# A recurrence and two dense layers on one core: a weight block loaded in halves, and a new order of the work

## The chip, the cores and the metric

The kernel runs on one core of a Trainium2 chip. The metric is device time in microseconds (us) of one execution; the time before is the median of three runs, 177.47 us (177.21 to 177.65). TensorE (PE) multiplies matrices into eight PSUM banks, VectorE (DVE), ScalarE (ACT) and GpSimd (POOL) do the elementwise work, and SyncE (SP) issues the transfers between the chip's memory (HBM) and the on-chip buffers (SBUF).

## The reference

```python
# q, k, v, f_logit: (4, 8, 768, 48) float32; w_in: (384, 2048); w_out: (2048, 384)
f = 1.0 / (1.0 + np.exp(-f_logit))
for t in range(S):
    state = f[:, :, t, :, None] * state + np.einsum('bhd,bhe->bhde', k[:, :, t], v[:, :, t])
    y[:, :, t] = np.einsum('bhd,bhde->bhe', q[:, :, t], state)
x = y.transpose(0, 2, 1, 3).reshape(B * S, H * D)      # (3072, 384)
h = x @ w_in
out = np.maximum(0.01 * h, h) @ w_out
```

The state of each of 32 heads decays by its own gate per element and step; the result goes through two dense layers with a leaky relu between.

## The kernel before

Time is cut into six chunks of 128 steps. The work comes in twelve units: units 0 to 3 are the first two chunks of one batch each (two steps in a pair share a row of the tiles), units 4 to 11 are one later chunk of two batches each. For each unit, and for each half `a` of it:

- f, k, q and v are loaded by SP (`Lf`, `Lk`, `Lq`, `Lv`; half a paired unit is 192 KB).
- ACT makes e = exp(-f) (`ge`, L229) and its logarithm lf (`gl`, L241); TensorE sums lf over time in PSUM (`cs`, L250 to L261); ACT makes the growth and decay factors em, at and end of it (`dec`, L274 to L280).
- DVE or POOL scale k and q by them (`k`, `q`, L286); v is cast on POOL (`v`, L291 to L300). TensorE turns k and q (`tk`, `tq`, L319), and DVE or ACT copy them out of PSUM (`ck`, `cq`); from unit 3 on a DMA transposes (`xk`, `xq`).
- TensorE makes the scores (`sc`, L355, L362), DVE masks them (`mk`, L372, L376), and TensorE mixes them with v and the last state (`mx`, `ms`, L393). The state's update is `pt` (L458, L463) on TensorE, `sf` (L473 to L480) on DVE, `sb` (L483) on POOL.
- ACT or DVE copy the mix out as xT (`xt`, L445, L447). TensorE multiplies it by w_in: `up` for one unit of 256 rows and 256 columns of w_in (six matmuls, L510), `uw` for a pair of units of 512 rows and 128 columns (three matmuls, L521). ACT applies the leaky relu (`pr` L516, `pw` L525); `dn` (L532) multiplies by a quarter of w_out, four matmuls at a time; the result is copied (`ob`) and stored (`st`).

Both weights are read in quarters into staging buffers, which are raw_fk4, raw_qv4, raw_fk5 and raw_qv5, the same that later hold the inputs of units 4 and 5, and cast to bfloat16 from there. `WI` and `WO` load a whole quarter (768 KB); `CI` and `CO` cast a third of it (128 x 512). `We_i_x` loads half x of w_in's quarter i (256 of its columns, 384 KB), and `Ce_i_x_y` casts 128 columns of it. A cast's last number is the engine: 0 DVE, 1 ACT, 2 POOL; elsewhere a last 1 is POOL (or ACT for copies out of PSUM).

All of this stands in one list of words, `order`, from L582 on; nothing else sets the order. Each word calls one of the functions in `parts`, and each engine runs its own words in the list's order, waiting for what they need; a word's bank of PSUM stands behind the @, so `up_0_4@6` is the fifth up of unit 0 into bank 6, which must have been read out by then. SP's words are its transfers in order. `F_n@b` puts n units of filler on TensorE (L135): two units are one matmul of 128 x 512 of a constant, an odd last one 128 x 256. Nobody reads them.

```python
    def fill(n, bank):
        for a in range(0, n, 2):
            m = 2 * min(2, n - a)
            nc.tensor.matmul(banks[bank][:, 0:128 * m].rearrange("t (a n) -> t a n", a=m), filler,
```

Of the kernel before, what the change touches and what calls it, by code (L numbers as in the profile page):

```python
# [15 lines left out]
def kernel(  # L16
# [665 lines left out]
```

## Time and profile before

| what | us |
|---|---|
| median of three runs | 177.47 (177.21 to 177.65) |
| the profiled execution | 176.78 |
| its span, first to last instruction | 175.0 |
| TensorE busy | 167.8 |
| ACT busy | 104.5 |
| DVE busy | 85.5 |
| POOL busy | 72.6 |
| fillers on TensorE (24 of 512 columns, 5 of 256) | 8.8 + 1.5 |

The page gives busy times per engine, the chain of work that ended last, and groups of instructions by line. A busy TensorE counts overlapping, pipelined matmuls, so a matmul's listed length is longer than its place in a row of them. The 1.78 us between the span and the time of the execution lie outside the instructions.

### The profile page before, as it was taken

The numbers are of one execution on the slowest core, as the hardware profiler recorded it, in microseconds if no ns is written. First come the engines' busy times: TensorE is split into PE (matmuls) and PEld (weight loads), VectorE is DVE, ScalarE is ACT, GpSimd is POOL, SyncE is SP. The second block draws the span as 40 slices with busy tenths as digits, with TensorE's granted clock in tenths as the row PEclk, the third lists the DMA queues.
The fourth block names the chain that finished last, engine by engine and source line by source line (L and its number), as shares of the span: only waits on it lengthen the run. The fifth ranks groups of instructions, "written<-read, shape, count | busy, mean of one in ns | idle before, by whom it ended". The sixth has DMA issues, their size and how long they took to land.

```text
span 175.0 us, 5158 instructions
## 1 busy us (share of the span) xinstructions
PE 167.8 (96%) x2101; PEld 105.6 (60%) x2101; DVE 85.5 (49%) x170; ACT 104.5 (60%) x228; POOL 72.6 (41%) x153
## 2 busy tenths in 40 slices
PE   7788899999999999999999999999999999999993
PEld 2555678887656776754555754566644565644672
DVE  4198886637439805761235680957720238600030
ACT  5873955899634681279963579910689910466501
POOL 7669776466701061530291646901601938000000
PEclk9999999999999999999999999999999999999999
DMA  5999999989999999988999999999989599040022
GB/s 142 267 284 312 358 307 328 365 265 280 202 186 179 123 236 194 184 184 175 229 220 145 267 194 189 208 148 205 246 183 228 109 194 276 9 184 0 0 90 90
DMA packets 110535, 34.93 MB, mean 200 GB/s; under 512 B 102960, under 2 KB 109744, under 8 KB 110512
## 3 DMA queue, kind: packets, MB, share of 16 engines
q1 hardware_dynamic: 110512, 34.61, 86.8%
q8 instruction: 16, 0.26, 0.6%
q14 instruction: 7, 0.06, 0.1%
HBM read 25.17 MB, written 4.72 MB: 171 GB/s over the span
## 4 chain that ended last, share of the span: by engine, by line
PE 85%; SPq 5%; DMA 3%; DVE 3%; issue 1%; POOL 0%; ACT 0%; POOLq 0%; DVEq 0%
PE ps L532 35%; PE ps L521 24%; PE ps L510 11%; SPq L164 5%; PE ps L393 5%; DMA raw_qv<-in_q_dram 3%; PE ps L362 3%; PE ps L548 2%; PE ps L258 1%; PE ps L463 1%; DVE wm L372 1%; PE ps L319 1%; DVE kh L286 1%; PE ps L355 1%; PE ps L261 1%
## 5 line engine op out<-in xcount | busy, mean ns | idle before, releaser
L532 PE MATMUL ps<-w_out,gT 128*128 128x384 bf16 x368 | 65.5, 326 | 0.0
L532 PEld LDWEIGHTS <-gT 128*128 128x128 bf16 x368 | 34.4, 98 | 23.0
L521 PE MATMUL ps<-xT,w_in 128*128 128x512 bf16 x192 | 44.1, 379 | 0.0
L525 ACT ACTIVATE gT<-ps 128x512 bf16<-128x512 f32 x64 | 35.1, 629 | 8.2 <-PE ps L521 7.9
L521 PEld LDWEIGHTS <-w_in 128*128 128x128 bf16 x192 | 18.3, 98 | 20.3 <-issue 0.2
L376 DVE TENSOR_TENSOR wm<-ps,ut 128x512 bf16<-128x512 f32 x32 | 19.9, 684 | 14.4 <-PE ps L362 8.2
L510 PE MATMUL ps<-xT,w_in 128*128 128x256 bf16 x192 | 22.8, 273 | 0.0
L445 ACT CAST xT<-ps 128x384 bf16<-128x384 f32 x13 | 6.3, 520 | 25.8 <-PE ps L393 25.8
L543 DVE COPY osb<-ps 128x384 f32<-128x384 f32 x15 | 8.2, 555 | 26.5 <-PE ps L532 21.7
L291 POOL CAST vb<-raw_qv 128x384 bf16<-128x384 f32 (+1 forms) x16 | 11.0, 690 | 24.5 <-DMA raw_qv<-in_v_dram 21.7
L516 ACT ACTIVATE gT<-ps 128x512 bf16<-128x512 f32 x32 | 17.3, 623 | 5.0 <-PE ps L510 5.0
L510 PEld LDWEIGHTS <-w_in 128*128 128x128 bf16 x192 | 18.2, 98 | 2.6
L286 DVE TENSOR_TENSOR qh<-raw_qv,at 128x768 bf16<-128x768 f32 (+1 forms) x10 | 9.4, 944 | 19.0 <-DMA raw_qv<-in_q_dram 16.4
L286 POOL TENSOR_TENSOR kh<-raw_fk,em 128x768 bf16<-128x768 f32 (+1 forms) x6 | 10.6, 1759 | 17.9 <-ACT em L274 9.6
L483 POOL CAST sb<-sf 64x192 bf16<-64x192 f32 x40 | 14.1, 353 | 8.8 <-DVE sf L473 6.7
L274 ACT ACTIVATE em<-ps 128x384 bf16<-128x384 f32 x24 | 12.7, 530 | 7.8 <-PE ps L261 7.0
L229 ACT ACTIVATE e<-raw_fk 128x384 f32<-128x384 f32 (+1 forms) x16 | 10.8, 683 | 9.8 <-DMA raw_fk<-in_f_logit_dram 9.8
L475 DVE TENSOR_TENSOR sf<-sf,ps 64x192 f32<-64x192 f32 x32 | 11.2, 351 | 5.4 <-PE ps L463 4.5
L286 DVE TENSOR_TENSOR kh<-raw_fk,em 128x384 bf16<-128x384 f32 (+1 forms) x10 | 8.2, 825 | 9.7 <-ACT em L274 9.5
L275 ACT ACTIVATE at<-ps 128x384 bf16<-128x384 f32 x24 | 12.9, 536 | 0.0
L286 POOL TENSOR_TENSOR qh<-raw_qv,at 128x384 bf16<-128x384 f32 (+1 forms) x6 | 7.6, 1259 | 11.5 <-DMA raw_qv<-in_q_dram 9.1
L480 POOL TENSOR_TENSOR sf<-sf,end 128x192 f32<-128x192 f32 x16 | 9.2, 573 | 7.4 <-ACT gT L525 5.9
(88 smaller groups left out, 191.4 us busy)
## 6 DMA issues: line engine op xcount, KB each, us to landing
out_dram<-osb SPq DMA_DIRECT2D x23, 192.0 KB, 2.6
raw_fk<-in_f_logit_dram SPq DMA_DIRECT2D x22, 192.0 KB, 3.9
raw_qv<-in_v_dram SPq DMA_DIRECT2D x22, 192.0 KB, 3.9
raw_fk<-in_k_dram SPq DMA_DIRECT2D x22, 192.0 KB, 4.1
raw_qv<-in_q_dram SPq DMA_DIRECT2D x22, 192.0 KB, 4.1
raw_fk<-in_moe_w_out_dram SPq DMA_DIRECT2D x2, 768.0 KB, 8.8
raw_qv<-in_moe_w_out_dram SPq DMA_DIRECT2D x2, 768.0 KB, 7.3
raw_fk<-in_moe_w_in_dram SPq DMA_DIRECT2D x1, 768.0 KB, 5.9
```

The lines of the kernel that those rows point to most:

```text
L274: nc.scalar.activation(ems[j % 2][:, a], t[:, 0:H * D], AF.Exp, scale=1.0)
L275: nc.scalar.activation(ats[j % 2][:, a], t[:, 0:H * D], AF.Exp, scale=-1.0)
L286: eng.tensor_mul(heads(j, to[j % NR], a)[:, :, :, 0:D], raw_heads(j, x, a), decays(j, by, a))
L291: nc.gpsimd.tensor_copy(out=heads(j, vb, a), in_=raw_heads(j, "v", a))
L376: nc.vector.tensor_mul(w, src.rearrange("t (p n) -> t p n", p=P2), ut[:, None, :].to_broadcast([128, P2, 128]))
L475: nc.vector.tensor_add(sf[rows], sf[rows], new)
L483: nc.gpsimd.tensor_copy(out=sb[rows, :, y * D:y * D + D], in_=sf[rows])
L510: nc.tensor.matmul(pm[:, i, :], w_in_of(ff, kk), xTs[j // 2 % 2][:, kk, j % 2].rearrange("t a s -> t (a s)"), start=(kk == 0), stop=(kk == ...
L516: nc.scalar.activation(dst, pm, AF.Prelu, alpha=0.01)
L521: nc.tensor.matmul(banks[bank], w_in_of(ff, kk), xTs[j // 2 % 2][:, kk].rearrange("t u a s -> t (u a s)"), start=(kk == 0), stop=(kk == NK ...
L525: nc.scalar.activation(g_blocks(j)[ff], banks[st[j].pop(("pm", ff))], AF.Prelu, alpha=0.01)
L532: nc.tensor.matmul(po, g_of(j, ff, a), w_out_b[quarter][:, ff % 4, :], start=(ff == 0), stop=(ff == NF - 1))
```

## The change

Only the list `order` changes; the functions are the same. The third quarter of w_in (`WI_2`, cast by `CI_2_x`) is now loaded in two halves and cast in four pieces, and its first half is the first of all weights to be loaded:

```diff
-WI_2
-CI_2_0_2 CI_2_1_2 CI_2_2_1
+We_2_0 We_2_1
+Ce_2_0_1_2 Ce_2_0_0_1 Ce_2_1_0_2 Ce_2_1_1_2
```

(These words are gathered here from their places in the list.) The rest of the list is drawn anew: the same words of every other kind and in the same numbers, in another order, with other banks and with some scalings, copies and casts on other engines. Six of 16 scalings of k were POOL's and now eight are; of q six were and now three. The pair mask goes from POOL to DVE. The fillers shrink from 53 units to 41:

```diff
-F_19@1 F_4@2 F_1@4 F_2@0 F_4@5 F_6@6 F_2@5 F_4@6 F_2@5 F_4@3 F_2@2 F_1@7 F_1@4 F_1@1
+F_15@1 F_2@3 F_2@5 F_3@1 F_1@2 F_2@6 F_1@0 F_1@0 F_6@6 F_4@0 F_1@0 F_1@2 F_1@4 F_1@2
```

The start of the list:

```diff
     order = """
-    c0 Lf_0_1 ge_0_1 Lf_0_0 Lv_0_1 Lf_1_1 gl_0_1 Lk_0_1 Lq_0_1 zk_1 zk_0 F_19@1 cs_0_1@0 zk_2 zv_2_0 ge_0_0 gl_0_0
-    Lv_0_0 dec_0_1 zv_0_0 ge_1_1 Lk_0_0 zv_1_0 q_0_1_0 Lq_0_0 zs_2_1 pm_1 gl_1_1 k_0_1_0 F_4@2 cs_0_0@1 cs_1_1@2
-    F_1@4 tq_0_1@3 Lf_1_0 Lk_1_1 Lq_1_1 tk_0_1@4 zs_1_1 dec_0_0 v_0_1 Lk_1_0 dec_1_1 Lv_1_1 ge_1_0 v_0_0 q_1_1_1
-    Lv_1_0 cq_0_1_1 k_0_0_0 Lf_2_0 Lq_1_0 q_0_0_0 tk_0_0@5 gl_1_0 Lf_2_1 ck_0_0_0 ck_0_1_0 WI_2 F_2@0 pt_0_2@6.7
-    v_1_1 v_1_0 sf_0_0 tq_0_0@0 zs_0_1 k_1_1_0 F_4@5 sc_0_1@1.2 cs_1_0@5 cq_0_0_1 tk_1_1@4 mk_0_1_1 F_6@6 tq_1_1@3
-    Lq_2_1 dec_1_0 mk_0_1_0 sc_0_0@6.0 q_1_0_1 sb_0_0 k_1_0_0 We_0_0 mk_0_0_1 We_1_1 mk_0_0_0 Lk_2_1 cq_1_1_0 ge_2_1
...
+    c0 zv_0_0 Lf_0_1 Lf_0_0 ge_0_1 Lk_0_1 Lf_1_1 gl_0_1 zk_0 Lq_0_1 Lk_0_0 Lq_1_1 F_15@1 cs_0_1@0 ge_0_0 zk_1 pm_0
+    gl_0_0 Lq_0_0 zs_2_0 zs_3_1 dec_0_1 k_0_1_0 Lf_2_1 ge_1_1 Lv_0_0 cs_0_0@1 Lf_1_0 Lv_0_1 Lf_2_0 Lk_1_1 dec_0_0
+    gl_1_1 q_0_1_0 q_0_0_1 We_2_0 Lk_1_0 Lq_1_0 Lv_1_0 Lv_1_1 F_2@3 tk_0_1@2 tq_0_1@3 ge_2_1 Lk_2_1 gl_2_1 k_0_0_0
+    zk_2 F_2@5 tk_0_0@4 zs_1_0 cq_0_1_0 cs_1_1@5 dec_1_1 ck_0_0_0 ck_0_1_0 ge_1_0 Lq_2_0 v_0_0 We_2_1 tq_0_0@6
+    cq_0_0_0 F_3@1 sc_0_1@7.0 sc_0_0@1.3 q_1_1_0 ge_2_0 v_0_1 k_1_1_1 mk_0_1_0 F_1@2 cs_2_1@4 We_0_0 gl_1_0 F_2@6
+    cs_1_0@2 mk_0_0_0 pt_0_2@6.5 tq_1_1@7 Lk_2_0 dec_1_0 Lv_2_1 We_1_0 k_1_0_1 mk_0_1_1 mk_0_0_1 cq_1_1_0 gl_2_0
```

What moves, at the three places that the prediction speaks of. First SP's loads, from the ninth or so on; raw_fk0 to raw_fk3 and raw_qv0 to raw_qv3 are the inputs of units 0 to 3, raw_fk5 is the staging buffer of w_in's third quarter, raw_fk4 and raw_qv4 those of the first and second. Before:

```order
L164 DMA raw_qv1_71<-in_v_dram 128x4x96 x2
L164 DMA raw_fk2_66<-in_f_logit_dram 128x4x96
L164 DMA raw_qv1_71<-in_q_dram 128x4x96
L164 DMA raw_fk2_66<-in_f_logit_dram 128x4x96
L173 DMA raw_fk5_69<-in_moe_w_in_dram 128x3x512
L164 DMA raw_qv2_72<-in_q_dram 128x4x96
L180 DMA raw_fk4_68<-in_moe_w_in_dram 128x3x256
L180 DMA raw_qv4_74<-in_moe_w_in_dram 128x3x256
L164 DMA raw_fk2_66<-in_k_dram 128x4x96 x2
```

With the change:

```order
L164 DMA raw_qv0_70<-in_v_dram 128x4x96
L164 DMA raw_fk1_65<-in_f_logit_dram 128x4x96
L164 DMA raw_qv0_70<-in_v_dram 128x4x96
L164 DMA raw_fk2_66<-in_f_logit_dram 128x4x96
L164 DMA raw_fk1_65<-in_k_dram 128x4x96
L180 DMA raw_fk5_69<-in_moe_w_in_dram 128x3x256
L164 DMA raw_fk1_65<-in_k_dram 128x4x96
L164 DMA raw_qv1_71<-in_q_dram 128x4x96
L164 DMA raw_qv1_71<-in_v_dram 128x4x96 x2
L164 DMA raw_fk2_66<-in_k_dram 128x4x96
L164 DMA raw_qv2_72<-in_q_dram 128x4x96
L180 DMA raw_fk5_69<-in_moe_w_in_dram 128x3x256
```

The whole third quarter stood behind both f of unit 2; now its first half stands ahead of unit 1's second k and q, unit 1's v and unit 2's first k and q go ahead of the second half, and both f of unit 2 stand ahead of all of these.

Second, ACT in the first stage: e and lf of a unit, em, at and end; ps0 to ps7 are the PSUM banks; lf1 is unit 1's logarithm, lf2 unit 2's. Before:

```order
L274 ACTIVATE em1_88<-ps2_157 128x384
L275 ACTIVATE at1_90<-ps2_157 128x384
L277 ACTIVATE end1_92<-ps2_157 128x2x2
L229 ACTIVATE e1_77<-raw_fk1_65 128x384
L332 COPY qT0_103<-ps3_158 128x2x256
L241 ACTIVATE lf1_79<-e1_77 128x4x2x48
L332 COPY qT0_103<-ps0_155 128x2x256
L274 ACTIVATE em1_88<-ps5_160 128x384
L275 ACTIVATE at1_90<-ps5_160 128x384
L277 ACTIVATE end1_92<-ps5_160 128x2x2
L229 ACTIVATE e0_76<-raw_fk2_66 128x384 x2
```

With the change:

```order
L274 ACTIVATE em1_88<-ps5_160 128x384
L275 ACTIVATE at1_90<-ps5_160 128x384
L277 ACTIVATE end1_92<-ps5_160 128x2x2
L229 ACTIVATE e1_77<-raw_fk1_65 128x384
L229 ACTIVATE e0_76<-raw_fk2_66 128x384
L241 ACTIVATE lf1_79<-e1_77 128x4x2x48
L274 ACTIVATE em1_88<-ps2_157 128x384
L275 ACTIVATE at1_90<-ps2_157 128x384
L277 ACTIVATE end1_92<-ps2_157 128x2x2
L241 ACTIVATE lf2_80<-e0_76 128x4x2x48
L332 COPY kT1_102<-ps1_156 128x2x256
```

Before, unit 1's second gate and logarithm (e1, lf1) stood ahead of everything of unit 2; now a gate of unit 2 (e0 from raw_fk2) stands between them.

Third, ACT between the first and the second layer's work: gT0 to gT23 are the relu's results, raw_fk3 is unit 3's f. Before:

```order
L516 ACTIVATE gT8_135<-ps5_160 128x512
L516 ACTIVATE gT12_139<-ps1_156 128x512
L516 ACTIVATE gT13_140<-ps4_159 128x512
L516 ACTIVATE gT0_127<-ps6_161 128x512
L516 ACTIVATE gT2_129<-ps2_157 128x512
L516 ACTIVATE gT11_138<-ps3_158 128x512
L200 CAST w_in3_174<-raw_qv5_75 128x512
L229 ACTIVATE e1_77<-raw_fk3_67 128x384
```

With the change:

```order
L187 CAST w_in1_172<-raw_qv4_74 128x3x128
L445 CAST xT1_126<-ps3_158 128x3x2x64
L229 ACTIVATE e1_77<-raw_fk3_67 128x384
L241 ACTIVATE lf0_78<-e1_77 128x4x2x48
L229 ACTIVATE e1_77<-raw_fk3_67 128x384
L516 ACTIVATE gT0_127<-ps0_155 128x512
L516 ACTIVATE gT1_128<-ps6_161 128x512
L241 ACTIVATE lf0_78<-e1_77 128x4x2x48
L516 ACTIVATE gT7_134<-ps3_158 128x512
L516 ACTIVATE gT17_144<-ps2_157 128x512
```

The relu of unit 0's first block (gT0) stood ahead of unit 3's first gate; now it stands behind both of unit 3's gates and one logarithm.

More of the change, by code (lines that the diff above doesn't have):

```diff
@@ new lines @@
+    cq_2_0_0 F_1@4 tk_2_0@3 ck_2_1_0 Ce_1_0_1_1 Lf_3_2 v_2_1 up_1_5@4 q_2_1_0 ck_2_0_1 up_1_2@6 tq_2_1@2 pr_0_5
+    pr_1_2 sf_1_1 Ce_0_1_0_2 sc_2_0@3.7 up_0_2@1 pr_1_0 cq_2_1_1 Ce_0_1_1_1 WO_2 mk_2_0_0 mk_2_0_1 pt_2_2@6.5
+    sc_2_1@3.2 pr_0_2 sf_2_0 up_1_4@7 up_1_1@1 pr_1_1 mk_2_1_1 up_0_1@6 sb_1_1 CI_3_2_2 sb_2_0 mk_2_1_0 CI_3_0_0
+    Ce_1_1_0_1 Ce_1_1_1_0 F_1@2 mx_2_2@2.3 WO_0 CI_3_1_2 ms_2 CO_2_0_2 xt_2_1_1 sf_2_1 ge_3_1 CO_2_2_2 CO_0_1_2
+    gl_3_1 ge_3_0 up_1_3@1 xt_2_0_0 pr_0_0 pr_0_1 up_0_6@5 CO_2_1_0 up_0_7@3 Lk_3_2 up_2_1@2 up_2_0@0 WO_1 Lf_5_0
@@ new lines @@
+    Lk_4_1 Lq_4_0 dn_1_1_3 dn_0_0_3 dn_2_0_1 dn_1_0_1 v_3_1 v_3_0 pr_2_7 pr_2_4 dec_5_1 ob_1_1_0 sc_3_0@6.1
+    sc_3_1@3.5 dn_1_0_2 mk_3_0_1 ob_0_0_1 pt_3_2@0.1 dn_0_1_2 mk_3_1_1 cs_5_0@5 dn_1_0_3 dn_0_1_3 ge_4_2 gl_4_2
+    mk_3_0_0 sf_3_0 mk_3_1_0 dec_5_0 sb_3_0 ob_1_0_0 mx_3_2@6.0 ms_3 ob_0_1_0 cs_4_1@3 xt_3_0_0 xt_3_1_1 sf_3_1
+    q_5_2_0 dn_2_1_0@5 cs_4_0@7 dec_4_1 up_3_0@2 dec_4_0 pr_3_0 up_3_1@6 up_3_2@0 k_5_2_1 up_3_3@1 up_3_6@3 dn_2_1_1
+    up_3_5@7 q_4_2_0 pr_3_1 pr_3_2 xk_5 Lk_4_0 xq_5 xq_4 st_0_1 pr_3_6 pr_3_3 Lv_5_1 k_4_2_1 st_0_0 dn_3_0_0@2
@@ new lines @@
+    up_3_7@6 up_3_4@0 dn_2_1_2 Lv_5_0 xk_4 Lv_4_1 Lv_4_0 pr_3_4 Lf_6_0 Lf_6_1 Lq_6_1 Lf_7_0 Lf_7_1 pr_3_5 Lk_6_1
+    Lf_9_1 sb_3_1 Lk_7_1 dn_2_1_3 sc_5_1@3.1 sc_5_0@0.7 dn_2_0_2 Lq_7_0 Lq_6_0 Lf_9_0 Lq_7_1 Lk_6_0 Lk_7_0 mk_5_0_1
+    Lv_6_1 st_1_1 st_1_0 pr_3_7 ob_2_1_0 v_5_2 mk_5_0_0 mk_5_1_0 mk_5_1_1 dn_3_1_0@6 dn_3_1_1 dn_3_0_1 dn_3_0_2
+    dn_2_0_3 pt_5_1@7 sc_4_0@5.0 sc_4_1@3.1 sf_5_1 mk_4_0_1 v_4_2 mk_4_1_1 dn_3_1_2 dn_3_1_3 mk_4_0_0 pt_5_0@7
+    mx_5_0@0 mx_5_1@1 mx_4_0@5 ob_2_0_1 xt_4_0_1 xt_5_1_1 mk_4_1_0 mx_4_1@4 xt_5_0_0 dn_3_0_3 pt_4_1@3 xt_4_1_0
```

101 lines of the change are left out of this document (43 added, 58 removed).

## Prediction

> **What bounds the kernel now.** I read the page's busy table first, then TensorE's waits in two windows, then the chain of waits in order of time.
>
> ```profile
> PE 167.8 (96%) x2101; PEld 105.6 (60%) x2101; DVE 85.5 (49%) x170; ACT 104.5 (60%) x228; POOL 72.6 (41%) x153
> PEclk9999999999999999999999999999999999999999
> PE ps L250 <- ACT lf L241: 1.1, 1, 1.1
> ```
>
> TensorE is busy 96% of the span, and the one wait shown is the longest of six that it has between 0 and 40 us; the same view from 40 us on lists none. The chain in order of time (start, length, what):
>
> ```profile
> 18.47 0.22 PE ps L135
> ...
> 24.59 0.40 PE ps L319 x4
> 24.99 1.97 PE ps L510 x18
> 26.95 0.11 PE ps L135
> ...
> 27.94 0.22 PE ps L319 x4
> ...
> 28.82 0.11 PE ps L135
> 28.93 0.57 PE ps L355 x32
> ...
> 32.23 0.45 PE ps L458 x16
> ...
> 34.74 1.02 PE ps L393 x73
> ...
> 169.44 2.65 PE ps L548 x32
> ```
>
> It runs through TensorE without a hole from 24.59 to 172.09 us. So behind 25 us the kernel is as long as TensorE's list of work. A change gains by having more of that list done by then or by taking fillers (L135) out of the part behind, and loses by putting a wait into it. Prices there: an up (six L510 matmuls) 1.97/3 = 0.66 us, a turn (L319 x4) 0.22, a filler of 256 columns 0.11, of 512 0.22, a pair of scores 0.57, unit states 0.45, a whole mix 1.02.
>
> **Fillers.**
>
> ```profile
> 1.05 4.23 PE L135 MATMUL ps<-filler 128*128 128x512 bf16 x10 [1.05 <-DVE filler L93]
> 5.08 0.37 PE L250 MATMUL ps<-lf,bu 128*128 128x192 bf16 x1
> 20.75 2.13 PE L510 MATMUL ps<-xT,w_in 128*128 128x256 bf16 x18
> 3.94 0.52 ACT L241 ACTIVATE lf<-e 128x384 bf16<-128x384 f32 x1
> 4.37 0.51 ACT L229 ACTIVATE e<-raw_fk 128x384 f32<-128x384 f32 x1
> ```
>
> The first ten fillers take 4.23 us, about 0.42 each, later ones 0.22: TensorE starts at half rate, though the granted clock says 1.00. The first cumulative sum needs lf, ready at 3.94 + 0.52 = 4.46, but stands behind the fillers until 5.08. With 15 units for 19, two matmuls fewer, they end near 4.3 and it starts at 4.46: 0.6 us earlier, worth little, since the next steps wait for loads. Of the 12 units dropped, only what stood behind 25 us is sure gain: two fillers of 0.11 before (26.95, 28.82), one in the change.
>
> **Loads and halves.** The first stage runs on a train of loads (SP's issue; issue to landing; who waited for a landing):
>
> ```profile
> 8.54 0.55 SPq L164 DMA_DIRECT2D raw_fk<-in_k_dram  x1
> raw_fk<-in_k_dram SPq DMA_DIRECT2D x1, 192.0 KB, 4.0
> raw_qv<-in_q_dram SPq DMA_DIRECT2D x1, 192.0 KB, 5.1
> 10.34 0.52 ACT L229 ACTIVATE e<-raw_fk 128x384 f32<-128x384 f32 x1 [0.92 <-DMA raw_fk<-in_f_logit_dram]
> 18.57 1.16 POOL L202 CAST w_in<-raw_fk 128x512 bf16<-128x512 f32 x2 [0.84 <-DMA raw_fk<-in_moe_w_in_dram]
> 32.06 0.52 ACT L229 ACTIVATE e<-raw_fk 128x384 f32<-128x384 f32 x1 [0.17 <-DMA raw_fk<-in_f_logit_dram]
> ```
>
> Counted in units of 192 KB, the 10th lands at 10.3, the 13th at 8.54 + 4.0 = 12.55, the third quarter (ending with the 22nd) at 18.5, the last f of unit 3 (42nd) at 32.05: (32.05 - 10.3)/32 = 0.68 us per unit, which I keep, the bytes being the same. In the change the first half of the third quarter is units 15 and 16 and lands near 14.5, its second half (24th) near 19.7. Before, the first up came at 20.75, with its weights' casts begun at 18.57 and the last xT behind them on ACT; so the halves alone shorten nothing, they give places 17 to 22 of the train to units 1 and 2.
>
> The work that makes room, with its prices:
>
> ```profile
> L372 DVE TENSOR_TENSOR wm<-ps,pair_mask 128x512 bf16<-128x512 f32 x16 | 10.2, 684 | 0.9 <-PE ps L355 0.9
> L286 POOL TENSOR_TENSOR kh<-raw_fk,em 128x384 bf16<-128x384 f32 x1 | 0.9, 910 | 0.3 <-DMA raw_fk<-in_k_dram 0.3
> L286 POOL TENSOR_TENSOR qh<-raw_qv,at 128x384 bf16<-128x384 f32 x4 | 4.3, 1068 | 3.9 <-DMA raw_qv<-in_q_dram 1.5 <-ACT gT L516 1.4 <-ACT xT L445 0.8
> L189 POOL CAST w_in<-raw_qv 128x384 bf16<-128x384 f32 x3 | 1.5, 506 | 0.2 <-DMA raw_qv<-in_moe_w_in_dram 0.2
> L120 POOL COPY pair_mask<-bu 64x64 bf16<-64x64 bf16 x6 | 1.3, 235 | 0.0
> 7.99 0.56 DVE L286 TENSOR_TENSOR qh<-raw_qv,at 128x384 bf16<-128x384 f32 x1 [5.30 <-DMA raw_qv<-in_q_dram]
> 39.08 0.55 ACT L274 ACTIVATE em<-ps 128x384 bf16<-128x384 f32 x1
> 39.87 2.15 ACT L516 ACTIVATE gT<-ps 128x512 bf16<-128x512 f32 x4
> ```
>
> Four half casts (0.51 each, three on POOL, one on ACT) stand for three casts (1.16/2): 0.3 us more, in work that TensorE doesn't wait for below. One more issue costs SP 0.55 while it waits for landings anyway. The pair mask goes to DVE, idle for 5.30 us until 7.99: covered there; uncovered, 8 x 0.24 at POOL's price.
>
> **The new order up to 25 us.** ACT now has unit 2's second gate ahead of unit 1's last logarithm, so that waits for the 13th unit: gate from 12.55, steps 0.43 apart (3.94 to 4.37), logarithm done at 13.5, cumulative sum on TensorE 13.55 to 14.0, TensorE idle for some 1.6 us before it. Behind it: unit 0's states to 14.45, a turn, DVE's copy of it to 15.1, sf to 15.85, a memset, an addition and a scaling to 17.1. Unit 0's mix runs at 15.1 (its masks, 0.65 apart, end at 14.6). Unit 1's four masks stand on DVE from 18.2 to 20.75. The first up starts at 20.25, when ACT has its xT; unit 1's mix at 20.9. Then DVE's sf to 21.5, POOL's sb to 22.2, the state part of the mix to 22.6, a turn, an up to 23.5. POOL's two scalings of k (0.91 each) end at 23.6 and 24.5 and let the next two turns go; from there no wait is left. At 24.9 the change has done four ups and eleven turns; before, at 24.82 (the turn of 24.59 over), three (20.75, x18) and ten, all else alike. So 0.66 + 0.22 + 0.11 for the filler = 0.99, minus 0.08 for the later moment: **0.9 us**. Both ends: the two scalings at 1.07 for 0.91 cost 0.3; the 13th unit 0.3 earlier gives 0.3.
>
> **Behind 25 us** I take 0.15 for unit 2's second scores, which wait for an ACT copy behind two relus, and 0.15 for knock-on. That leaves **0.6 us**; without these 0.9, with twice as much 0.3.
>
> **Rivals.** (a) *PSUM banks eat the gain.* In the change ACT has two gates and a logarithm of unit 3 ahead of the relu of unit 0's first block, and the first waits for the 42nd unit, 32.05. From there ACT works without a pause: three steps of 0.43, then relus 0.54 apart (2.15/4); the first block's relu ends at 33.95, a later one of the same bank, behind eleven relus, a logarithm, two decays of 0.8 (39.08 to 39.87), two relus and a cast, at 43.4. TensorE, from 24.9, has ten ups, a turn, the scores, the states, a filler and the mix, 9.0 us, ahead of its claim to the first bank: 33.9, with the waits above 34.2. At the later one it comes at 43.4 too. So a landing or an ACT run half a microsecond later costs as much: 177.47 - 0.6 + 0.5 = 177.4. For it: slack of 0 to 0.3. Against it: before, ACT had 5.00 us of work in these 5, and TensorE did not wait (columns: TensorE busy, its loads, DVE, ACT, POOL):
>
> ```profile
> 35.00:40.00 5.00, 5.00 (x107) 4.39 (x91) 1.70 (x4) 5.00 (x15) 2.84 (x5) 1.00 0.85 257
> ```
>
> That the weights were never last, so that only the fillers' 0.11 counts, gives 177.4 too and goes with (a).
>
> (b) *Slower: the gate that waits for the 13th load.* If that transfer takes the 5.1 us of the q row for 4.0, unit 1's logarithm, its cumulative sum, DVE's whole train and the mix come 1.1 later, and TensorE, in order, with them. It decides from 0.6 us late on; at 1.1: 177.47 - 0.6 + 1.1 = 178.0. Against it: the k row had the 13th place.
>
> (c) *Slower: the clock.* The idle 1.6 us before 13.55, with fewer fillers around, drops TensorE to half rate. The work from there to unit 2's cumulative sum, some 3.7 us, would double until the rate returns, and the first rise took 4.3 us (fillers from 1.05; the matmuls of 5.08 are the last slow ones): 1.8 us late after some of it hides in waits, 178.7. Against it: before, the wait of 1.1 us cost no rate. [...]
>
> **How the numbers follow.** The profiled execution took 176.78 us (span 175.0), 0.7 below the median of 177.47; the forecast is 176.2 on its scale and 177.47 - 0.6 = 176.9 on the median's, which I give. Its own range, 176.2 to 177.2, comes from the ends above (0.9 + 0.3, and 0.3). Under 0.3% (0.53 us) counts as none. Forecast 0.50; (a) 0.20; (b) 0.20, 177.6 to 178.5; (c) 0.10. So faster 0.50, the same 0.20, slower 0.30. The whole range goes from 175.9, a further 0.3 for banks that nobody waits for, to 178.6.
>
> **What will show it.** Right: the first up near 20.3, unit 1's mix near 21, four ups done by 24.9, no TensorE wait behind 28 us. Wrong: TensorE waiting for ACT between 33 and 45 us (a); unit 1's last cumulative sum later than 13.6 (b); turns or fillers at twice their spacing behind 8 us (c). New waits in units 4 to 11, whose order was also drawn anew, would be wrong too: I price them at nothing, because the TensorE work between a unit's cumulative sums, scores, mix and ups stays within 3 us of before or grows.

## The result: slower, 179.1 us for 177.0

| | before | changed |
|---|---|---|
| median of 20 executions each | 177.01 us (176.24 to 179.48) | 179.09 us (177.12 to 181.31) |
| ratio of the times | 1 | 1.0062 (95% interval 1.0037 to 1.0088) |
| profiled execution | 176.78 us | 177.28 us |
| its span | 175.0 us | 175.3 us |
| time outside the span | 1.78 us | 1.98 us |

The ratio leaves out disturbed executions, of which the changed kernel has more, so it is nearer to 1 than the medians. The forecast was 176.9 us; the result is above its range (175.9 to 178.6). In two later batches, on two chips, the unaltered change had 178.21 and 177.82 us beside 176.55 and 176.82.

The profiled execution, 177.28 us, is the second shortest of the 20. Its busy table and clock:

```profile
PE 167.1 (95%) x2097; PEld 105.4 (60%) x2097; DVE 86.3 (49%) x181; ACT 107.1 (61%) x232; POOL 64.2 (37%) x139
PEclk9999999999999999999999999999999999999999
```

TensorE's waits over the whole span (who waited for whom, us in total, times, longest):

```profile
PE ps L250 <- ACT lf L241: 1.3, 1, 1.3
PE ps L135 <- DVE filler L93: 1.1, 1, 1.1
PE ps L319 <- POOL qh L286: 0.8, 1, 0.8
PE ps L319 <- DVE qh L286: 0.4, 1, 0.4
PE ps L510 <- ACT xT L445: 0.4, 1, 0.4
PE ps L355 <- ACT qT L332: 0.4, 1, 0.4
PE ps L362 <- DMA kT<-kh: 0.3, 1, 0.3
```

And TensorE's timeline (start, length, what, the idle time before it):

```profile
4.52 0.32 PE L250 MATMUL ps<-lf,bu 128*128 128x192 bf16 x1
...
13.00 0.24 PE L250 MATMUL ps<-lf,bu 128*128 128x192 bf16 x1 [1.28 <-ACT lf L241]
...
19.79 0.81 PE L510 MATMUL ps<-xT,w_in 128*128 128x256 bf16 x6
...
65.21 0.62 PE L362 MATMUL ps<-qT,kT 48*128 48x128 bf16 x16
...
96.55 0.62 PE L362 MATMUL ps<-qT,kT 48*128 48x128 bf16 x16 [0.26 <-DMA kT<-kh]
```

Up to the first up the forecast holds in this execution: the first cumulative sum at 4.52 (forecast 4.46, before 5.08), unit 1's last at 13.00 behind 1.28 us of idle time (13.55 and 1.6), the first up at 19.79 (20.25, before 20.75). Four ups and eleven turns are done at 25.0 (24.9), where before had three and ten.

Yet the kernel isn't faster. Four marks show where the lead goes. Up to each of them TensorE has done the same words in both lists, fillers aside (at unit 5's scores each list has one down group that the other has not yet):

| us | before | changed | again, e1 | again, e9 |
|---|---|---|---|---|
| first scores of unit 5 | 65.7 | 65.2 | 65.5 | 66.2 |
| first `uw` of units 4, 5 | 75.2 | 75.0 | 75.0 | 75.8 |
| first `uw` of units 10, 11 | 151.1 | 151.0 | 150.7 | 151.8 |
| last half downs (`dh`) | 169.3 | 169.2 | 168.8 | 169.9 |
| end of the span | 175.0 | 175.3 | 174.9 | 176.0 |
| time of the execution | 176.78 | 177.28 | 176.95 | 178.05 |

A lead of 0.5 us at 65 us in one execution is a lag of 0.5 in another, and from the last half downs to the end the execution (with what lies outside its span) takes 7.5 us before and 8.1 in all three of the change. Two things are to be explained, then: where the head's lead goes, and what costs 0.6 us behind the last work.

### The profile page after: what moved, and what is told of

It is laid out like the page before. It is cut to its first block, busy times and chain, and to the rows that moved or that the text cites. A ratio compares the mean times of both kernels' runs of the same rounds, so it can differ in the third digit from the quotient of the medians.

```text
span 175.3 us, 5153 instructions
## 1 busy us (share of the span) xinstructions
PE 167.1 (95%) x2097; PEld 105.4 (60%) x2097; DVE 86.3 (49%) x181; ACT 107.1 (61%) x232; POOL 64.2 (37%) x139
## 4 chain that ended last, share of the span: by engine, by line
PE 84%; SPq 6%; DMA 5%; ACT 2%; issue 1%; DVE 1%
PE ps L532 30%; PE ps L521 23%; PE ps L510 12%; PE ps L393 6%; SPq L164 4%; DMA kT<-kh 3%; DMA raw_fk<-in_f_logit_dram 2%; PE ps L362 2%; PE ps L548 2%; SPq L339 1%; PE ps L258 1%; PE ps L463 1%; PE ps L135 1%; PE ps L355 1%; PE ps L458 1%; PE ps L319 1%
## 5 line engine op out<-in xcount | busy, mean ns | idle before, releaser
L510 PE MATMUL ps<-xT,w_in 128*128 128x256 bf16 x192 | 23.8, 273 | 0.4 <-ACT xT L445 0.4
L286 DVE TENSOR_TENSOR qh<-raw_qv,at 128x768 bf16<-128x768 f32 (+1 forms) x13 | 11.5, 885 | 23.0 <-ACT at L275 11.6
L274 ACT ACTIVATE em<-ps 128x384 bf16<-128x384 f32 x24 | 12.1, 506 | 8.5 <-PE ps L261 7.5
L445 ACT CAST xT<-ps 128x384 bf16<-128x384 f32 x15 | 7.4, 527 | 15.9 <-PE ps L393 15.8
L286 POOL TENSOR_TENSOR kh<-raw_fk,em 128x384 bf16<-128x384 f32 (+1 forms) x8 | 10.8, 1350 | 12.1 <-DMA raw_fk<-in_k_dram 7.5
L275 ACT ACTIVATE at<-ps 128x384 bf16<-128x384 f32 x24 | 12.2, 509 | 0.0
L372 DVE TENSOR_TENSOR wm<-ps,pair_mask 128x512 bf16<-128x512 f32 x16 | 10.1, 684 | 3.1 <-PE ps L355 1.8
L241 ACT ACTIVATE lf<-e 128x384 bf16<-128x384 f32 (+1 forms) x16 | 11.2, 701 | 0.2
```

The source lines that it names most:

```text
L241: nc.scalar.activation(dst, src, AF.Ln, bias=1.0)
L274: nc.scalar.activation(ems[j % 2][:, a], t[:, 0:H * D], AF.Exp, scale=1.0)
L275: nc.scalar.activation(ats[j % 2][:, a], t[:, 0:H * D], AF.Exp, scale=-1.0)
L286: eng.tensor_mul(heads(j, to[j % NR], a)[:, :, :, 0:D], raw_heads(j, x, a), decays(j, by, a))
L510: nc.tensor.matmul(pm[:, i, :], w_in_of(ff, kk), xTs[j // 2 % 2][:, kk, j % 2].rearrange("t a s -> t (a s)"), start=(kk == 0), stop=(kk == ...
```

## The experiments

The medians below are in us, followed in brackets by the ratio to the kernel before and its 95% interval. The first theories: **A**, windows of TensorE's clock (stretches at half rate; e4's, 8.0 to 11.4 us, and e8's, 8.9 to 12.4, last about 3.4) in the first 25 us (the 20 executions list mean clocks of 0.98 to 0.99 in 12); **B**, scores of later units that wait for DMA transposes with no time to spare; **C**, jitter of the first stage's loads. Later came **T**, the order of the last downs and stores; **D**, work queued behind a weight load on ACT; **E**, **F** and **G**, the lengths of POOL's, DVE's and SP's instruction lists. Kernels of one batch share a chip and the executions of the kernel before.

### e1 to e4: again, two splices, filled holes

e1 is the changed kernel as it is. 

> The changed kernel, unaltered, for a second profile and for the spread of its times. Its first profile (177.28 us) is close to before's 176.78: the head gains 0.8 us as forecast, and the loss stands elsewhere or in executions that differ from that one. Theory A (clock: in many executions TensorE drops to half rate for one or two windows of 3.4 us in the first 25 us, where the change has holes of 0.8 and 1.3 us): the granted clock is below 0.995 in about half of the executions, and these are the slow ones; executions at 1.00 take 177.3. Theory B (units 6 to 11: scores wait for transposes with no slack): times spread from 177 to 179 at a clock of 1.00, and the profile shows TensorE waiting for kT or qT between 90 and 150 us. Theory C (loads of the first stage): times spread at a clock of 1.00, and the first up starts later than 20 us in a slow execution.

e2 is the changed list up to the first `uw` of units 4 and 5 (75 us) and the list of before from there. 

> The change's list up to the first up of units 4 and 5 (about 75 us), and before's list from there on. Theory B: the loss is gone, 0.3 to 0.8 us faster than before. Theories A and C: as slow as the change, ratio near 1.006.

e3 is the reverse. 

> Before's list up to the first up of units 4 and 5, and the change's list from there on. Theory B: slower than before by 0.5 to 1.5 us. Theories A and C: like before, within 0.3 us, apart from 0.35 us for the stores at the end.

e4 fills the holes ahead of 9.7 and 13.0 us, where TensorE stood idle for 0.84 and 1.28 us in the result's profile, and has 53 units again:

```diff
+F_4@1
 tq_0_0@6
...
-F_2@6
+F_10@6
 cs_1_0@2
```

> The changed kernel with 12 more units of filler: four ahead of unit 0's last turn of q and eight more ahead of unit 1's last cumulative sum, where TensorE stood idle for 0.84 and 1.28 us; 53 units in all, as many as before. Theory A: the granted clock is 1.00 in nearly all executions, and the time falls by 1 to 2 us, to before's or below. Theories B and C: the time stays, ratio near 1.006 to before.

Measured, beside 176.55 us: e1 178.21 (1.0105, 1.0074 to 1.0137), e2 181.83, e3 180.85, e4 178.34 (1.0123, 1.0089 to 1.0157). The splices say nothing on their parts: TensorE stands 3.1 us at the seam in each, since words that one list has ahead of the seam (a load of f, a store) come behind it in the other. In e4's profile both holes are gone, but the half rate runs from 8.0 to 11.4 us, ahead of them: e4 filled holes behind the window, and two of its six executions still have a clock of 0.987 or 0.99. The other four have a median of 178.27, so the time stays e1's without a window too; that speaks against A as the whole cause.

### e5 to e8: more time for units 4 and 7, the old tail, fewer fillers

```diff
e5: Lk_5_0 Lk_5_1 ... Lk_4_1 Lq_4_0 xk_5
+Lk_4_0   (behind Lk_4_1; k_4 earlier too; xk_4 behind xq_4, ahead of a store and two loads of v)
e6: as e5, and
+Lk_6_0 Lk_7_0   (ahead of Lq_7_0)   +k_6_2_0 xk_6   (ahead of pw_4_5)
+xk_7 q_7_2_0 xq_7   (behind k_7_2_0, ahead of Lv_7_0)
e7: the changed list up to uw_10, the list of before from there, with
+WI_2 CI_2_0_2 CI_2_1_2 CI_2_2_1   (at the seam, near 150 us)
e8: the list of before with
-F_19 F_4 F_1 F_2 F_4 F_6 F_2 F_4 F_2 F_4 F_2 F_1 F_1 F_1
+F_15 F_3 F_1 F_1 F_3 F_4 F_1 F_3 F_2 F_3 F_2 F_1 F_1 F_1
```

> The changed kernel with unit 4's last key load (Lk_4_0) put ahead of unit 5's transposes on SP's queue, and unit 4's kT transpose issued right behind its qT transpose instead of behind a store and two value loads; nothing else differs. In the three traces of the changed lists this transpose landed 0.2 to 0.4 us ahead of unit 4's scores (69.6 to 69.9 in the first), and one landing differed from another by up to 2 us (3.2 to 5.2 us). Theory B (transposes that land with no time to spare, so that executions whose DMAs take longer lose 1 to 2 us at full clock): the landing moves to about 66, 3 us ahead of the scores; if unit 4 is the main place, the median falls by 0.5 to 1.0 us against the unaltered changed kernel's 178.2. Theory A (half-rate clock windows set the median): no change, within 0.3 us. Theory T (only the tail and small stalls): no change.

> As the run before, and with unit 7 too: units 6 and 7's second key loads ahead of unit 9's gate load, kT of unit 6 and then kT of unit 7 transposed ahead of the value loads and of unit 7's qT. In the traces of the changed lists unit 7's last transpose landed 0.0 to 0.2 us ahead of its scores (96.5 and 96.6). Theory B: the landing moves to about 94.5, 2 us ahead, no wait of the scores near 96 is left, and the median falls to 177.0 to 177.4 with a spread as narrow as the kernel before had in its last session (176.05 to 177.85). Theory A: within 0.4 us of the unaltered kernel's 178.2, with the spread (176.95 to 179.1) unchanged. Theory T: 177.9.

> The changed kernel up to the last two units' first up projection (near 151 us), and the order of the kernel before from there on. Theory T: the profiles showed the last down projections 0.08 us earlier than before and the end 0.3 us later, so the tail cost 0.35 us: the median falls by 0.35 us against the unaltered changed kernel, to 177.8, and the time from the last half down projections (dh, near 169.3) to the end falls from 6.0 to 5.7 us. Theories A and B: the tail was one execution's accident, the median stays within 0.2 us of 178.2.

> The kernel before with its filler matmuls cut from 53 units to 41 at their own places (the first run of them from 19 to 15), and nothing else. Theory A: fewer fillers let the granted clock drop for a window in some of the executions, as the changed kernel showed in about half of its own (0.98 or 0.99 in the list of clocks), while the kernel before showed 0.998 to 1.0 in 11 of 11; the median rises by 0.5 to 1.5 us. Theories B and T: the clock stays at 0.998 or above and the time within 0.3 us of the kernel before, or up to 0.4 us less for the fillers that stood on TensorE's path.

Measured, beside 176.45 us: e5 180.42 (1.0207, 1.0174 to 1.0240), e6 180.33, e7 179.87, e8 176.44 (0.9997, 0.9974 to 1.0020).

e5 and e6 made a new wait: with the transpose ahead of the loads of v, the state product of unit 5 waits for its v. TensorE in e5, first its timeline, then windows of 2 us (length, TensorE busy, its loads, DVE, ACT, POOL, granted clock, DMA share, GB/s):

```profile
71.82 0.33 PE L463 MATMUL ps<-vb,kh 128*128 128x96 bf16 x4 [1.92 <-POOL vb L291]
```

```profile
70.00:72.00 2.00, 0.18 (x4) 0.18 (x3) 0.00 (x0) 0.42 (x1) 1.05 (x2) 1.00 1.17 232
72.00:74.00 2.00, 2.00 (x24) 1.18 (x22) 1.69 (x4) 0.00 (x0) 1.56 (x4) 0.58 1.24 231
74.00:76.00 2.00, 2.00 (x22) 1.06 (x23) 1.49 (x3) 0.00 (x0) 0.89 (x3) 0.57 1.08 207
```

A wait of 1.9 us, and then a granted clock of 0.58 and 0.57 through the next 4 us, some 1.7 us more by these two figures: the wait is paid nearly twice. e7 loads and casts w_in's third quarter a second time at its seam, because `WI_2` is a word that the changed list doesn't have; TensorE's two waits there, 1.45 and 0.40, are for these casts, and its median says nothing on T. (From the last half downs to the end it takes 6.3 us for 6.1.) e8 is the clean one: 12 units of filler less change nothing in the time. But 6 of its 12 executions show a clock of 0.99, while the 96 listed clocks of the kernel before, with 53 units, are all 0.997 or more. The windows of e8, and the same stretch before:

```profile
6.00:7.00 1.00, 0.28 (x7) 0.22 (x5) 0.00 (x0) 0.83 (x3) 0.95 (x4) 1.00 1.03 261
7.00:8.00 1.00, 0.31 (x4) 0.30 (x4) 0.15 (x1) 0.97 (x4) 0.09 (x1) 1.00 1.13 300
8.00:9.00 1.00, 0.86 (x13) 0.49 (x11) 0.88 (x2) 1.00 (x5) 0.59 (x1) 0.97 1.00 270
9.00:10.00 1.00, 0.83 (x7) 0.57 (x8) 0.91 (x2) 0.30 (x2) 1.00 (x3) 0.50 1.14 296
10.00:11.00 1.00, 1.00 (x19) 0.70 (x18) 0.88 (x3) 0.56 (x2) 0.33 (x1) 0.50 1.12 291
11.00:12.00 1.00, 1.00 (x13) 0.62 (x8) 0.69 (x3) 1.00 (x3) 0.19 (x1) 0.50 1.10 302
12.00:13.00 1.00, 1.00 (x22) 0.52 (x20) 0.97 (x2) 0.44 (x1) 0.81 (x2) 0.82 1.14 303
```

```profile
6.00:7.00 1.00, 0.70 (x10) 0.51 (x9) 0.00 (x0) 1.00 (x4) 0.96 (x4) 1.00 1.12 308
7.00:8.00 1.00, 0.18 (x3) 0.18 (x3) 0.01 (x1) 0.97 (x3) 0.07 (x1) 1.00 1.06 284
8.00:9.00 1.00, 0.92 (x13) 0.55 (x10) 1.00 (x2) 1.00 (x5) 0.47 (x1) 1.00 0.96 250
```

By the clock column the half rate lasts from 8.9 to 12.4 us. e8's executions with such a window have a median of 176.62, the others 176.34. So fewer fillers do cost clock, and in the head of this list a window costs some 0.3 us, which the shorter list gives back.

### e9 to e12: again, and time for units 4 and 5 by other moves

```diff
e10: -pt_5_1@7   (ahead of sc_4_0)   +dn_3_1_2
     +pt_5_1@7   (ahead of pt_5_0@7; sf_5_1 behind it)
e11: as e10, Lk_4_0 as in e5, and on SP
-xq_5 xq_4 st_0_1 Lv_5_1 st_0_0 Lv_5_0 xk_4 Lv_4_1 Lv_4_0
+xq_5 Lv_5_1 Lv_5_0 xq_4 xk_4 Lv_4_0 Lv_4_1 st_0_1 st_0_0
e12: as e11, with e6's moves for unit 7 and
+dn_10_1_3 ob_10_1_0 ... dn_11_0_2 dn_11_0_3 ob_11_0_0 ... dn_10_0_2 dn_10_0_3 dh_11_1_1 ... ob_10_0_0
```

> The changed kernel unaltered, beside the next three on one chip (its medians so far were 179.1 and 178.2 on two chips, so the next three are compared with this one). Theory B, narrowed by the traces: near 69 to 73 us the changed order has three hand-overs without slack, where the kernel before has 0.9 us or more: unit 5's first state products come ahead of unit 4's scores and start 0.2 us after their values are cast, unit 4's kT lands 0.3 us ahead of its scores, and unit 4's mix meets its values 0.0 us after their cast. Expected by every theory: 178 to 180 us, 0.5 to 1.5% slower than the kernel before, and in the profile, if it is a slow execution, a wait of TensorE of 0.3 us or more at L463, L362 or L393 between 69 and 74 us (theory B), or a clock below 1.0 in the first 25 us without such a wait (theory A).

> The changed kernel with two edits of TensorE's order near 69 us alone: unit 5's second state product (pt_5_1) goes from ahead of unit 4's scores to just ahead of the first one (pt_5_0), and one down group (dn_3_1_2, 0.66 us) comes ahead of unit 4's scores; its sum on VectorE moves with it. Loads and transposes stay as they are. Theory B: values get about 2 us of slack and unit 4's kT about 0.7 us, the median falls by 0.5 to 1.0 us against the unaltered changed kernel on the same chip. Theory A: no change, within 0.3 us.

> As the run before, and on SP's queue too: unit 4's last key load ahead of unit 5's transposes, unit 5's value loads right behind unit 5's transposes, unit 4's kT right behind its qT, its value loads next, and the two stores of unit 0 behind these. All of units 4 and 5's hand-overs then have 1.5 us or more. Theory B: the median is 0.8 to 1.5 us below the unaltered changed kernel on the same chip, 177 to 177.5, and the spread is within 2 us. Theory A: no change, within 0.4 us.

> As the run before, with unit 7's key loads and kT transpose earlier as in the run of units 4 and 7, and the last down groups in the order of the kernel before (one output tile finished and stored ahead of the last three, the last but one copied on VectorE instead of ScalarE), with nothing cut elsewhere. Theory B: the scores of unit 7 have 1 us of slack, another 0.2 to 0.5 us off the median. Theory T: the time from the last half down projections to the end falls from 6.0 to 5.7 us, 0.3 us off. Both: 176.3 to 177.0, even with the kernel before or up to 0.3 us under it. Theory A: as the unaltered kernel, less 0.3 us of the tail.

Measured, beside 176.82 us: e9 177.82 (1.0053, 1.0030 to 1.0076), e10 179.39 (1.0139, 1.0109 to 1.0169), e11 183.6, e12 183.2. e10's own flaw is plain in TensorE's timeline: the two state products have one bank, so the second waits for DVE to read the first:

```profile
74.57 0.33 PE L463 MATMUL ps<-vb,kh 128*128 128x96 bf16 x4 [1.48 <-DVE sf L475]
```

An estimate of e10 without this wait, 179.39 - 1.48 = 177.9 us, is the unaltered kernel's time: the added slack bought nothing that shows. e11 and e12 have the same wait (1.1 us) and more at the scores behind it, and windows of half rate there. Theory B is not confirmed by anything here, and e12, with the old order of the last downs, still takes 6.1 us from the last half downs to the end, which speaks against T.

e9's profile (178.05 us, clock 0.999) has what the first one hid. ACT's timeline there:

```profile
22.75 0.51 ACT L187 CAST w_in<-raw_fk 128x384 bf16<-128x384 f32 x1 [2.73 <-DMA raw_fk<-in_moe_w_in_dram]
23.16 1.03 ACT L445 CAST xT<-ps 128x384 bf16<-128x384 f32 x2
```

TensorE's:

```profile
20.07 0.81 PE L510 MATMUL ps<-xT,w_in 128*128 128x256 bf16 x6
...
23.31 0.28 PE L510 MATMUL ps<-xT,w_in 128*128 128x256 bf16 x1 [0.27 <-ACT w_in L187]
24.25 0.70 PE L510 MATMUL ps<-xT,w_in 128*128 128x256 bf16 x5 [0.65 <-ACT xT L445]
...
66.22 0.62 PE L362 MATMUL ps<-qT,kT 48*128 48x128 bf16 x16
```

ACT stands 2.73 us at a cast until its weights land. Unit 1's two xT copies queue behind it, and TensorE loses 0.27 + 0.65 = 0.92 us in one up, the third (its six matmuls are the x1 and the x5). Before, ACT's copies waited for the mix alone:

```profile
20.86 0.55 ACT L187 CAST w_in<-raw_fk 128x384 bf16<-128x384 f32 x1
...
23.75 1.04 ACT L445 CAST xT<-ps 128x384 bf16<-128x384 f32 x2 [0.90 <-PE ps L393]
```

The load is the first half of w_in's *first* quarter. It is SP's 21st load before, landing at 20.2 us (in e3, e15 and e18, which have the same head, at 21.0, 21.7 and 20.2), and the 23rd with the change, landing at 21.5 (profiled execution), 22.0 (e1) or 22.7 (e9).

### e13 to e18: the wait, the halves and the program's end taken singly

```diff
e13: -Ce_0_0_0_1 (ahead of xt_1_0_1 xt_1_1_1)   +Ce_0_0_0_1 (behind them)
e14: as e13, +pd_1 x14 near 150 us (a zeroing of one column on POOL)
e15: the list of before, +pd_0 x12 near 150 us (the same on DVE)
e16: the list of before with
-WI_2   -CI_2_0_2 CI_2_1_2 CI_2_2_1
+We_2_0 We_2_1   +Ce_2_0_0_2 Ce_2_0_1_2 Ce_2_1_0_2 Ce_2_1_1_1
e17: as e14, -up_0_0 up_1_0 ... up_1_5 ... up_1_4   +up_1_5 up_1_4 ... up_0_0 ... up_1_0   (and their relus)
e18: the list of before, units 6 to 9 stored in two pieces of 64 rows
```

> The changed kernel with one move on ScalarE: the cast of a piece of the first weight quarter (Ce_0_0_0_1) goes from ahead of unit 1's two xT copies to right behind them. In the trace of the unaltered changed kernel at 178.05 us, ScalarE stood 2.7 us at this cast until its weight load landed at 22.75 us, the two xT copies ran only then (23.16 to 24.2), and TensorE waited 0.65 us at 24.25 for them; the kernel before copied xT as soon as the mix was there. Theory D (the head's gain is given back by work that queues behind a weight load on ScalarE): the wait of L510 on xT near 24 us goes, unit 5's first scores come 0.4 to 0.7 us earlier than the 66.1 us that is the median over ten profiles of lists with the changed first 65 us, and the median falls by 0.4 to 0.7 us against the unaltered 177.8 to 178.2. Theory B (slack near 69 to 73 us): what is gained ahead of 65 us is lost there, the median stays within 0.2 us.

> As the run before, with 14 one-column zeroings of a scratch tile added to GpSimd's list near 150 us, where it has nothing left to do. In all nine profiles of lists that give GpSimd 198 records, the last semaphore step of the program on GpSimd starts 0.33 to 0.36 us after the drain ahead of it; in the five with 201 records or more (the kernel before has 216) it starts 0.04 us after. Theory E (the end of GpSimd's list is fetched late when the list is short or lies otherwise): with 212 records the hole is 0.04 us, and the median is 0.3 us below the run before. Rival: the hole has another cause, it stays at 0.33 and the time is the same.

> The kernel before with 12 one-column zeroings of a scratch tile added to VectorE's list near 150 us, where it is idle; nothing else differs. The time outside the profiled span (the execution's time less its span) was 1.73 to 1.90 us in all lists with 248 to 252 records on VectorE (the kernel before among them) and 1.95 to 2.13 us in all with 257 or more (the changed one). Theory F (the number of VectorE's instructions sets it): with 260 records the time outside is 2.0 us and the median 0.2 us above the kernel before. Rival (another engine's list, SyncE's above all, which is longer in the same kernels): it stays 1.8 us and the time is the same.

> The kernel before with the first part of the change alone: the third weight quarter loaded and cast in halves at the places of its whole load and casts (two loads for one, four casts for three), with the order and the 53 filler units of before. Theories B, D, E: the change's loss comes from the new order, not from the halves: within 0.3 us of the kernel before (176.5 to 176.8 on two chips). Rival: the halves themselves cost (one more load on the queue, smaller pieces), 0.3 us or more slower, with first up projections later than 20.75 us.

> The changed kernel with unit 1's xT copies ahead of the weight cast on ScalarE and the 14 zeroings on GpSimd, as two runs before, and with the ups taken in the order in which their weights arrive: up_1_5 and up_1_4 (third weight quarter, there since 20 us) change places with up_0_0 and up_1_0 (first quarter, whose half landed at 21.5 to 22.7 us in the changed lists and at 20.2 us in the kernel before). Theory D, mended by the run with xT first, where TensorE waited 0.9 us for that weight's cast instead: no wait of L510 above 0.3 us is left ahead of 26 us, unit 5's first scores come at 65.4 us or earlier, and the median is 0.4 to 0.8 us below the 177.75 of the run with the zeroings. Theory B: the median stays within 0.2 us of 177.75.

> The kernel before with the eight stores of units 6 to 9 in two pieces of 64 rows each, so that SyncE's list is 8 DMAs longer (205 records or more instead of 197), late in the program where its queue has room. The time outside the profiled span was 1.73 to 1.90 us in all lists with 197 to 200 records on SyncE and 1.95 to 2.13 us in all with 201 or 202; VectorE's count was ruled out by the run before. Theory G (the length of SyncE's list sets it): the time outside is 2.0 us, and the median 0.2 us above the kernel before. Rival: it stays 1.8 us.

| us | median | ratio to before | outside the span, mean |
|---|---|---|---|
| e13 | 178.25 | 1.0087 (1.0057 to 1.0118) | 2.02 |
| e14 | 177.75 | 1.0070 (1.0040 to 1.0099) | 2.00 |
| e15 | 176.45 | 0.9997 (0.9974 to 1.0021) | 1.78 |
| e16 | 176.51 | 1.0002 (0.9983 to 1.0020) | 1.78 |
| e17 | 177.97 | 1.0053 (1.0020 to 1.0086) | 2.01 |
| e18 | 177.03 | 1.0015 (0.9988 to 1.0041) | 1.81 |

e13 to e16 stand beside 176.59, e17 and e18 beside 176.84.

e13: the copies come first now, and TensorE waits for the weights themselves, which land as late as in e9. From its list of waits:

```profile
PE ps L510 <- ACT w_in L187: 0.9, 1, 0.9
```

So in e9 and e13 the late half was a cause of the wait, whether by the queue on ACT or directly. e17 lets two ups of unit 1, whose weights are there, go first. Unit 5's scores come at 65.6 us, in e13 at 66.2 and in e14 at 66.1 (one profile each), and the fastest of its 12 executions, 176.29, is within 0.2 us of the fastest of before on that chip (176.11). But the median stays, and its profile shows the next waits, and what released ACT's copies (its lines stand two further on, so L364 is the scores, L447 the xT copies and L512 the ups):

```profile
PE ps L364 <- DMA kT<-kh: 0.8, 1, 0.8
PE ps L512 <- ACT xT L447: 0.5, 1, 0.5
22.44 1.04 ACT L447 CAST xT<-ps 128x384 bf16<-128x384 f32 x2 [2.55 <-PE ps L512]
```

The wait for xT is left with the weights in place. By the last line the two copies start when the second up is done (22.41), take 1.04 us, and the third up waits for them. In e13, in e14 and in the result's own profile they also start 0.03 to 0.04 us behind that up; in e1 they come 0.15 us behind it and in e9 0.7. So 0.4 to 0.5 us of the wait belongs to the copies' place between the two ups, and the late half adds 0 (the result's profile) to 0.5 (e9). Theory D is half right: the late half is there, but its cost is smaller than the theory says, and curing it does not bring the median back.

e14 settles the end. The last steps of the program on POOL, by kernel (duration min/median/max in ns, first and last start). Before:

```profile
L677 POOLq EVENT_SEMAPHORE  x4: 17/17/17, 174.3 to 174.9; - x4
L677 POOLq DRAIN  x3: 34/78/1202, 147.7 to 174.7; - x3
```

Changed:

```profile
L677 POOLq EVENT_SEMAPHORE  x4: 17/17/17, 174.3 to 175.2; - x4
L677 POOLq DRAIN  x3: 34/78/1204, 147.0 to 174.7; - x3
```

e14:

```profile
L681 POOLq EVENT_SEMAPHORE  x4: 17/17/17, 175.2 to 175.7; - x4
L681 POOLq DRAIN  x3: 34/78/182, 150.9 to 175.6; - x3
```

Both programs have the first of these semaphore steps at 174.3 and the last drain at 174.7; the last semaphore step comes at 174.9 before and at 175.2 with the change. Between the last drain and the next step the records show 0.04 us before and 0.34 changed. With 14 more instructions on POOL the hole is gone. In all ten profiles of lists with 198 records on POOL it is there, 0.33 to 0.36 us, ahead of the 197th; e7, with 201, has it (0.37 us) three steps sooner, again ahead of the 197th. (e14's expectation counted e7 among the lists without a hole; it had moved.) From the last half downs to the end of the span these ten take 6.07 to 6.10 us, and the nine with 205 records or more 5.71 to 5.79. Among the nine is e3, with the change's own order of the end (5.73), so T fell, and the 0.3 us are this hole's. The change took POOL from 216 records to 198.

e15 and e18 rule out the lengths of DVE's and SP's lists as the cause of the 0.2 us outside the span, which stays open. e16 rules out the halves.

## Why the prediction was wrong

The forecast was a gain of 0.6 us, and the change is slower. Two terms of its sum failed, the head's gain and the end that was put at nothing, and a rival at 0.10 was there in nearly half of the executions.

- **"0.66 + 0.22 + 0.11 ... 0.9 us" in the head, 0.6 after the knock-on: this gain isn't there in a typical execution.** In the profiled one it is: the first ups, turns and mixes stood within 0.5 us of their places, the lead at 65 us was 0.5, and "the halves alone shorten nothing" holds too (e16). But that one is the second shortest of 20, and its agreement is in part luck. At 65 us, six profiles with the changed list up to there lie at 65.2 to 66.3, median 65.8 (the result's, e1, e2, e7, e9, e10), and four with the list of before (its own, e3, e15, e18) at 65.6 to 66.3, median 66.0: 0.2 us, less than either spread. (Theory C, a jitter of the change's own, falls with it: before has the same spread.) Even 0.2 flatters the change, since the profiled executions of e15 and e18 are 1.2 and 0.7 us above their medians, and those of the result and e1 1.8 and 1.3 us below theirs. An estimate for typical executions: from unit 5's scores to the end of the execution the profiles take 111.1 to 111.5 us before (its own, e15, e18) and 111.5 to 112.1 with the change (the result's, e1, e9). The means of these, taken off the medians of the three batches (the change's at full clock), put the scores at 65.2 to 65.7 us before and at 65.5 to 66.6 with the change: 0 to 0.9 us later, where the forecast had 0.6 earlier.
- **"A turn, an up to 23.5 ... from there no wait is left": the step in it that is known to be wrong.** This third up waits 0.4 us (the result's profile) to 0.9 (e9), for the xT copies and for the first half of the first quarter, which the new train brings at 21.5 to 22.9 us in the six profiles above, and the old one at 20.2 to 21.7 in the four. I followed the train for the third quarter and for unit 1, and not for this up. It isn't the whole of the loss: without the late half's part (e17) the median stays.
- **The program's end, not in the sum at all.** I called the 1.78 us outside the span fixed and took nothing for what follows the last work. It costs 0.3 us inside the span (the hole on POOL, shown by e14) and 0.2 outside.
- **Rival (c), the clock, at 0.10.** Of 38 executions of the unaltered change 17 have a mean clock under 0.996; of before none in 96. Its premise, fewer fillers, was right (e8: a clock of 0.99 in 6 of 12 executions). Its place was not: in e4, e5 and e13 the half rate begins at 7.5 to 8.0 us, ahead of the hole at 13 us that it named. What spoke against it, before's wait of 1.1 us at a granted clock of 1.00, does not carry over to other lists: in the 3.4 us ahead of the fall the longest idle piece is 1.41 us in e8 and 0.52 in e5, both shorter than its 1.6. Its price, 1.8 us, is not settled. By batch, the executions with a lowered clock have medians 2.0, 1.2 and 0.7 us above the others; but in e8 a window in the head cost 0.3, and e4, e5 and e13, which have one, come to unit 5's scores at 66.0, 65.3 and 66.2 us, like the profiles without. What makes 179 to 181 us, perhaps windows behind waits as in e5, no profile of the unaltered kernel caught. The range, up to 178.6, left out this rival's own 178.7.
- **Rival (a), ACT and the banks.** No wait of TensorE for ACT between 33 and 45 us; it fell. Rival (b): unit 1's last cumulative sum came at 13.0, so it fell too (13.35 at the latest in the other five profiles).
- **"New waits in units 4 to 11 ... at nothing."** One was there, 0.3 us at 96.5 us, and unit 7's transposes are as late before (e16 waited 0.4 there). From 75 to 169 us the profiles agree within 0.3 us, so this step holds.

The executions at full clock have medians 0.5 to 1.3 us above before, by batch. The end is 0.5 of this; the rest stands ahead of 65 us by the estimate above, and its cause stays open. The likeliest reading, that the new order meets more loads just in time and so varies more, was only argued: e5, e6 and e10 to e12 tried to give slack behind 65 us and made waits of their own. No version beat the kernel before.

## What to carry to other kernels

When transfers trade places, follow the ones that moved back to their first user, and look for what queues behind that user on its engine (in e9 two copies of ACT stood behind a cast that waited 2.73 us for its load). Judge an order by several profiles at marks with equal work done, since a single one can show a lead that the median has not (0.5 us at 65 us here, in an execution 1.8 us below its median). The end of the program had its own cost here: with POOL's records down from 216 to 198 it took 0.3 us more inside the span, and 0.2 us more outside for a cause that stays open; the edit was forecast to gain 0.6.

## What the runs showed of the hardware

- POOL stops for 0.33 to 0.37 us ahead of its 197th record in all eleven profiles in which this record is one of the program's last steps, and 14 instructions more on POOL end it (e14, e17). That the stop belongs to this place in any list is not shown: in e14 and e17 the 197th record is one of the added zeroings and follows the one ahead of it after 0.06 us, like the others. In e14 (2.16 us for 14 of 0.10 us):

```profile
148.82 2.16 POOL L584 MEMSET pad_g<- 128x1 bf16 x14
```

  What POOL waits for the trace doesn't say; the late fetch in e14's theory E is not shown.
- TensorE's clock fell to half rate behind short idle pieces: in e8 (above) the longest in the 3.4 us ahead of the fall is 1.41 us; in e5, whose windows follow, it is 0.52, and TensorE is busy for some 60% of the 3.4 us. By the clock column the half rate lasts about 3.4 us in both (8.9 to 12.4 and 7.5 to 10.9). All twenty traces together have twelve falls ahead of the program's last steps (two each in e5, e11 and e12, one each in e2, e3, e4, e6, e8 and e13), each behind a piece of 3.4 us with TensorE busy for 9 to 61% by its records and no idle stretch over 3.1 us; seven pieces of 46 to 60% kept the full rate (before: 1.75 us busy from 6.5 to 9.9; changed: 2.03 from 9.0 to 12.4), and so did every one above 61%. So in these traces a low busy share goes with the falls but does not decide them alone.

```profile
4.00:5.00 1.00, 0.76 (x10) 0.57 (x9) 0.00 (x0) 0.97 (x3) 0.00 (x0) 1.00 0.99 243
5.00:6.00 1.00, 0.60 (x14) 0.53 (x10) 0.12 (x1) 1.00 (x3) 0.00 (x0) 1.00 1.13 294
6.00:7.00 1.00, 0.72 (x10) 0.24 (x5) 0.65 (x2) 1.00 (x5) 0.00 (x0) 1.00 1.13 310
7.00:8.00 1.00, 0.60 (x5) 0.45 (x6) 0.96 (x3) 0.93 (x4) 0.00 (x0) 0.73 1.13 304
8.00:9.00 1.00, 1.00 (x8) 0.86 (x8) 1.00 (x7) 0.00 (x0) 0.36 (x1) 0.50 1.13 313
```
